# Both halves of a first operand over two hardware queues, and a new written order

## The chip, the cores and the metric

One core of a Trainium2 chip runs the kernel. The metric is the device time of one execution in microseconds (us). The times below are of eleven runs of the kernel before; one of them was also profiled.

## The reference

The reference is a two-step attention followed by a feed-forward layer. With q, k and v of 8 batches, 8 heads, 576 rows and 64 columns, and 32 packed rows p in each head:

```python
p_packed = softmax(p @ k.T / 8) @ v          # 32 rows per head
attn = softmax(q @ p_packed.T / 8) @ p_packed # 576 rows per head
x = attn, heads side by side                  # 4608 x 512
h = x @ w_in                                  # 512 -> 2048
out = (s * relu(h) ** 2 + b) @ w_out          # 2048 -> 512
```

Inputs and output are float32 in DRAM; the kernel's matmuls work on bf16.

## The kernel before

Inputs come in through DMAs. POOL's queue casts float32 to bf16 on the way. For each batch the work on TensorE (PE) is: transposes of k, q and p by matmuls with an identity (for later batches DMA transposes issued by SP); first scores (`s`), whose exponentials (`e`, on ACT) are the first softmax; the packed product (`a`, tile `pp`, copied to `ppc` on DVE); second scores (`c`) with their exponentials; their sums and reciprocals (`w`: matmuls with ones, then Ln and Exp on ACT as `ld` and `rcd`, then a product on DVE into `aT`); the product of the packed rows and w_in (`e`, `f`, `E`: four concurrent column groups, then scaled copies into `pw`, one half by ACT and one by DVE for `e`, both by DVE for `f`); the first layer (`h` and `m`: matmuls of `pw` and `aT`, Relu on ACT into `rlu`, square on DVE into `gT`); and the second layer (`t`: two of the 16 matmuls that add up one output tile of 128 rows, `yps`, which DVE copies into `ysb` with the factor and the bias, and SP stores).

The first three batches are not a loop. A string, `ORDER`, lists words by hand, and a dictionary, `words` (line 732 and after), says what each does. An instruction keeps its place on its engine (`tc.keep_in_program_order`), so the string sets the order on PE, ACT, DVE, POOL and SP. A word with numbers names the batch and the part: `kT.0.1` is the transpose of the second half of k of batch 0, `h.0.4` one of sixteen half results of the first layer of batch 0, `t.3` two matmuls of output tile 3, `win.0` the two DMAs of one quarter of w_in, `wout.0` one of w_out, `qh.0.0` two DMAs of q. `z` is an idle matmul: 128x512 zeros into a PSUM tile that nobody reads (`idle`, line 234). `pp2` doubles p in SBUF, `mask` makes the identity on POOL, `k.1`, `q.1`, `v.1` load later batches.

`four` and `three` change how PSUM is shared. At first there are two rings of two tiles, each two banks. From `four` on one ring holds four running sums (three output tiles and the sum of w_out, words `b`), and the other serves everything else. At `three` both rings are closed and replaced by three tiles of two banks and two of one bank for the output. After the string comes a loop over batches 3 to 7, with later loads, transposes and packed work at fixed steps.

Batch 0's k is loaded in two ways. Its first half (heads 0 to 3) is word `kf`: SP's hardware queue brings it as float32 into a corner of `gT`, which is not used yet, and word `kc` casts it, two heads by DVE and two by ACT. Its second half is `kh.0.1`, cast on the way by POOL's queue:

```python
    def load_first_k():
        kn[0] = raw("kn", 0).rearrange("r (h x) -> r h x", h=H)
        sp.dma_start(out=first_k, in_=k[0, 0:4].rearrange("h (r c) d -> r h (c d)", c=NC))
    def cast_first_k():
        vec.tensor_copy(out=kn[0][:, 0:2, :], in_=first_k[:, 0:2, :])
        act.copy(out=kn[0][:, 2:4, :], in_=first_k[:, 2:4, :])
```

Line 104 is the helper through which DVE, ACT, POOL and SP issue everything, line 93 that of matmuls and line 96 that of transposes, so the profile's groups are told apart by their tiles.

Of the kernel before, what the change touches and what calls it, by code (L numbers as in the profile page):

```python
# [7 lines left out]
F32 = mybir.dt.float32  # L8
# [4 lines left out]


ORDER = """
z kf kc kh.0.1 mask p.0.1 qh.0.0 qh.0.1 kT.0.1 kT.0.0 z z v.0 z win.0 win.1 pp2.0.1 pT.0 qT.0.1 z
s.0.0 s.0.1 qT.0.0 win.2 a.0.0 a.0.1 c.0.0 f.0.0 z win.3 c.0.1 z w.0.0 z w.0.1 e.0.1 z z h.0.2 h.0.0
e.0.2 wout.0 q.1 h.0.4 h.0.7 h.0.5 e.0.3 h.0.6 h.0.8 wout.1 h.0.1 h.0.11 h.0.13 k.1 h.0.3 four
h.0.10 t.1 p.1.2 h.0.9 wout.2 t.2 h.0.15 qT.1.1 t.1 t.2 qT.1.0 b.0 t.0 h.0.12 t.0 v.1 b.1 pp2.1.2
t.1 kT.1.1 t.2 pT.1 wout.3 sb b.2 h.0.14 q.2 kT.1.0 t.1 t.0 t.0 b.3 s.1.0 s.1.1 t.0 t.1 k.2 t.1  # L20
p.2.8 a.1.0 b.4 a.1.1 q.3 b.5 b.6 b.7 c.1 t.1 t.0 t.1 e.1.0 w.1.0 t.0 t.0 w.1.1 v.3 t.2 qT.2.1 t.2
e.1.1 k.3 t.2 t.2 t.2 kT.2.0 pp2.2.8 m.1.0 three t.3 t.3 pT.2 kT.2.1 f.1.2 t.3 e.1.3 v.2 t.3 qT.2.0
t.3 m.1.8 m.1.1 m.1.6 m.1.14 m.1.13 m.1.3 t.3 m.1.5 m.1.10 qo.3 m.1.2 t.4 qD.3 s.2.0 m.1.7 m.1.9
m.1.11 t.4 s.2.1 m.1.4 m.1.12 kD.3 t.3 m.1.15 a.2.0 t.4 a.2.1 t.4 t.4 t.4 pT.3 k.4 c.2 t.4 t.4 t.3
E.2.0 w.2.0 t.6 t.6 t.5 w.2.1 t.6 t.5 t.5 vo.3 t.6 E.2.1 t.6 m.2.5 t.5 t.5 t.6 pT.4 t.6 s.3.0 s.3.1
t.6 m.2.1 t.5 m.2.3 a.3.0 m.2.13 t.5 m.2.10 a.3.1 t.7 q.4 t.7 t.7 c.3 t.5 qo.4 m.2.2 t.7 t.7 w.3.0
t.8 t.8 E.3.0 qD.4 t.8 t.8 kD.4 w.3.1 v.4 t.7 m.2.14 t.7 m.2.0 m.2.15 m.2.6 m.2.7 m.2.9 t.8 t.8
m.2.12 m.2.8 m.2.11 t.7 m.2.4 E.3.1 t.8 t.8 vo.4
"""

@with_exitstack
def kernel(
# [19 lines left out]
    nc = tc.nc  # L52

    B, H, S, D = q.shape
# [6 lines left out]
    R = 96  # L61
    NC = S // R
# [43 lines left out]
    vec, act, pool, sp = (Pinned(e) for e in (nc.vector, nc.scalar, nc.gpsimd, nc.sync))  # L106
# [8 lines left out]
    kn, qn, vn = {}, {}, {}  # L115
# [7 lines left out]
    def raw(name, b):  # L123
        if (name, b - 1) in mine and b > 3:
            mine[name, b] = mine[name, b - 1]
        else:
            mine[name, b] = spare.pop(0)
        return bufs[mine[name, b]][:]
# [32 lines left out]
    def load_chunks(store, src, b, tag, hf):  # L161

        if hf == 0:
            store[b] = raw(tag, b).rearrange("r (h x) -> r h x", h=H)
        w = CP * D
        pool.dma_start(
            out=store[b][:, :, hf * w:(hf + 1) * w],
            in_=src[b].rearrange("h (r c) d -> r h (c d)", c=NC)[:, :, hf * w:(hf + 1) * w],
        )
# [3 lines left out]
    gT = wpool.tile([P, NFF, 3 * S], BF16, name="gT")  # L173
# [16 lines left out]
            in_=moe_w_out[m0 * P:m1 * P, :].rearrange("(m p) d -> p m d", p=P),  # L190
        )

    first_k = gT[0:R, 0:2, :].rearrange("p m s -> p (m s)")[:, 0:8 * NC * D].bitcast(F32)
    first_k = first_k.rearrange("r (h x) -> r h x", h=4)

    def load_first_k():

        kn[0] = raw("kn", 0).rearrange("r (h x) -> r h x", h=H)
        sp.dma_start(out=first_k, in_=k[0, 0:4].rearrange("h (r c) d -> r h (c d)", c=NC))

    def cast_first_k():
        vec.tensor_copy(out=kn[0][:, 0:2, :], in_=first_k[:, 0:2, :])
        act.copy(out=kn[0][:, 2:4, :], in_=first_k[:, 2:4, :])


    identb = constp.tile([P, P], BF16, name="identb")
# [2 lines left out]
    vec.memset(zeros[:], 0.0)  # L209
    svec = constp.tile([P, 1], F32, name="svec")  # L210
    bvec = constp.tile([P, 1], F32, name="bvec")
    nc.scalar.preload_act_table_set("natural_log_exp_and_others")
    KW = H * HS + 32
    kT = [constp.tile([P, KW], BF16, name=f"kT{i}") for i in range(2)]
    qT = [constp.tile([P, NC, HP, R], BF16, name=f"qT{i}") for i in range(2)]
# [511 lines left out]
    def constants():  # L727
# [9 lines left out]
        "qh": lambda b, x: load_pairs(qn, q, b, "qn", x),  # L737
        "vh": lambda b, x: load_pairs(vn, v, b, "vn", x),
        "qc": lambda b, x: load_chunks(qn, q, b, "qn", x),
        "kf": load_first_k,  # L740
        "kc": cast_first_k,
        "p": lambda b0, b1: load_p(b0, min(b1, B)),
        "win": load_w_in,
# [33 lines left out]
    for b in range(3, B):  # L777
        a = b + 1
        c = a + 1
# [61 lines left out]
```

The softmax here doesn't subtract the row's maximum and nothing guards it: scores larger than these inputs give would overflow.

## Time and profile before

| | us |
|---|---|
| median of 11 runs | 254.76 |
| lowest and highest | 254.37, 256.61 |
| the profiled execution | 256.38 |
| its span | 254.60 |
| PE busy | 242.0 (95%) |
| DVE busy | 145.7 (57%) |
| ACT busy | 143.6 (56%) |
| POOL busy | 32.9 (13%) |

Eight of the eleven times lie between 254.37 and 254.98, three between 256.10 and 256.61. The profiled execution is one of the three. Its time is 1.78 us more than its span, which is the part that the profile shows.

A busy PE is not a PE at its peak: the page counts an instruction as busy from its start to its modelled end, whatever the clock. The row PEclk gives the granted clock in tenths of full speed. A row of the chain of waits gives a start, a length and the work that ran or was waited for. In the timeline a bracket at the end of a row gives the idle time of its engine ahead of it, and what ended it.

### The profile page before, as it was taken

What the parts mean: (1) busy time and instruction counts of PE and PEld (TensorE: products, weight loads), DVE (VectorE), ACT (ScalarE), POOL (GpSimd) and SP (SyncE); (2) the same over time, 40 slices, a digit from 0 to 9 for tenths busy, and PEclk for the clock granted to TensorE, in tenths of its full rate; (3) what the DMA queues carried; (4) which work ended last, traced back from release to release, by engine and by line L of the source; (5) the groups of instructions that cost most, each with busy time, mean ns of one, the idle gap of its engine ahead of it and who ended that gap; (6) DMA issues with size and microseconds to landing.
All of it is one profiled execution on the core that took longest, in us unless ns stands there. A gap on an engine that the chain in (4) does not pass through costs nothing.

```text
span 254.6 us, 5632 instructions
## 1 busy us (share of the span) xinstructions
PE 242.0 (95%) x2330; PEld 138.0 (54%) x2330; DVE 145.7 (57%) x301; ACT 143.6 (56%) x220; POOL 32.9 (13%) x49
## 2 busy tenths in 40 slices
PE   0789999999999999999999999999999999999994
PEld 0554665456745656655566555645565555555443
DVE  3345843498757568667844677367834564454221
ACT  3058943457946698758663775568645764543000
POOL 8745242100003001100020013000000000000000
PEclk9986999999999999999999999999999999999999
DMA  7999999999499976995899499918511113111332
GB/s 142 194 202 205 205 204 194 196 234 209 83 122 163 215 138 113 169 232 121 154 138 223 103 172 147 213 47 157 115 41 44 41 47 82 41 41 41 85 82 82
DMA packets 54634, 34.61 MB, mean 136 GB/s; under 512 B 27344, under 2 KB 50128, under 8 KB 54608
## 3 DMA queue, kind: packets, MB, share of 16 engines
q0 software_dynamic: 24928, 18.32, 48.5%
q1 hardware_dynamic: 29584, 15.87, 27.7%
q8 instruction: 18, 0.29, 0.5%
q14 instruction: 8, 0.07, 0.1%
q10 hardware_dynamic: 96, 0.07, 0.1%
HBM read 37.23 MB, written 9.44 MB: 183 GB/s over the span
## 4 chain that ended last, share of the span: by engine, by line
PE 92%; DMA 3%; ACT 2%; DVE 1%; issue 1%; POOLq 0%
PE yps L93 51%; PE hps L93 37%; PE hps L96 3%; DMA raw<-in_k_dram 3%; ACT rlu L104 1%; ACT e L104 1%; DVE ysb L104 0%; ACT pw L104 0%; DVE pw L104 0%; DVE ppc L104 0%; POOLq L104 0%; POOLq L825 0%
## 5 line engine op out<-in xcount | busy, mean ns | idle before, releaser
L93 PE MATMUL yps<-w_out_sb,gT 128*128 128x512 bf16 (+2 forms) x592 | 144.6, 374 | 0.2 <-DVE ysb L104 0.2
L104 ACT ACTIVATE rlu<-hps 128x576 bf16<-128x576 f32 x128 | 80.6, 654 | 58.3 <-PE hps L93 52.1
L104 DVE TENSOR_TENSOR gT<-rlu 128x576 bf16<-128x576 bf16 x128 | 58.3, 457 | 56.9 <-ACT rlu L104 54.8
L93 PE MATMUL hps<-aT,pw 128*128 128x288 bf16 x512 | 80.2, 287 | 0.3 <-DVE pw L104 0.2
L93 PEld LDWEIGHTS <-gT 128*128 128x128 bf16 x592 | 53.5, 98 | 49.7 <-issue 7.2
L93 PEld LDWEIGHTS <-pw 128*128 128x128 bf16 x512 | 49.8, 98 | 32.2 <-issue 0.8
L104 DVE SCALAR_TENSOR_TENSOR ysb<-yps,svec,biasrep 128x512 f32<-128x512 f32 (+2 forms) x37 | 27.0, 732 | 16.5 <-PE yps L93 16.4
L104 DVE TENSOR_SCALAR pw<-hps,rd 128x1024 bf16<-128x1024 f32 (+1 forms) x22 | 22.6, 1037 | 1.0 <-PE hps L93 0.4
L104 ACT ACTIVATE pw<-hps,rd 128x1024 bf16<-128x1024 f32 (+1 forms) x18 | 17.5, 975 | 3.8 <-PE hps L93 3.7
L104 DVE TENSOR_TENSOR aT<-e,rcd 128x576 bf16<-128x576 bf16 x16 | 12.1, 758 | 11.1 <-ACT rcd L104 11.0
L104 POOL DMA_DIRECT2D raw<-in_k_dram x8 | 6.3, 782 | 87.9 <-DMA kT<-raw 62.8
L104 ACT ACTIVATE e<-hps,rs 128x576 bf16<-128x576 f32 (+1 forms) x18 | 11.4, 686 | 10.7 <-PE hps L93 8.7
L96 PE MATMUL hps<-identb,raw 96*64 96x96 bf16 (+1 forms) x216 | 9.5, 224 | 6.0 <-DMA raw<-in_k_dram 6.0
L104 ACT ACTIVATE e<-hps 96x768 bf16<-96x768 f32 x16 | 12.5, 801 | 3.9 <-PE hps L93 3.9
L96 PEld LDWEIGHTS <-raw 96*64 96x64 bf16 (+1 forms) x216 | 8.1, 117 | 8.8 <-DMA raw<-in_k_dram 6.5
L93 PE MATMUL hps<-w_in_sb,ppc 64*32 64x512 bf16 x256 | 11.2, 397 | 0.1
L104 ACT ACTIVATE rcd<-ld 128x576 f32<-128x576 f32 x16 | 11.0, 685 | 0.5
L104 ACT ACTIVATE ld<-hps 128x576 f32<-128x576 f32 x16 | 10.3, 643 | 1.0 <-PE hps L93 0.9
L104 DVE COPY raw<-raw 96x1536 bf16<-96x1536 bf16 x20 | 10.4, 562 | 0.0
L93 PEld LDWEIGHTS <-raw 96*64 96x64 bf16 (+1 forms) x264 | 7.7, 106 | 2.7 <-issue 2.0
L93 PE MATMUL hps<-e,raw 96*64 96x32 bf16 (+1 forms) x264 | 8.7, 188 | 0.4 <-ACT e L104 0.4
L104 POOL DMA_DIRECT2D raw<-in_q_dram x11 | 8.5, 784 | 4.0 <-PE hps L93 2.5
(45 smaller groups left out, 105.3 us busy)
## 6 DMA issues: line engine op xcount, KB each, us to landing
raw<-in_v_dram POOLq DMA_DIRECT2D x8, 576.0 KB, 11.6
out_dram<-ysb SPq DMA_DIRECT2D x23, 192.0 KB, 3.4
raw<-in_q_dram POOLq DMA_DIRECT2D x7, 576.0 KB, 11.0
raw<-in_k_dram POOLq DMA_DIRECT2D x7, 576.0 KB, 8.9
out_dram<-ysb SPq DMA_DIRECT2D x24, 128.0 KB, 2.4
w_in_sb<-in_moe_w_in_dram POOLq DMA_DIRECT2D x8, 256.0 KB, 10.0
w_out_sb<-in_moe_w_out_dram POOLq DMA_DIRECT2D x4, 512.0 KB, 15.2
out_dram<-ysb SPq DMA_DIRECT2D x23, 64.0 KB, 3.1
```

Source lines behind the costliest of these rows:

```text
L93: return tc.keep_in_program_order(nc.tensor.matmul(*a, **kw))
L96: return tc.keep_in_program_order(nc.tensor.transpose(*a, **kw))
L104: return lambda *a, **kw: tc.keep_in_program_order(f(*a, **kw))
```

## The change

Both halves of batch 0's k are loaded as float32, the first by SP's hardware queue and the second by ACT's, into two corners of `gT`. The two loads are issued ahead of all other words, and ahead of the load of ACT's table. The cast becomes a word with a half, `kc.0` and `kc.1`, each with one DVE and one ACT instruction. `kf` and `kh.0.1` are gone from the string. The string is otherwise a new order of the same words, with three `z` instead of ten, and with `e.1.2 f.1.3` instead of `f.1.2 e.1.3` (another quarter of `pw` is scaled by DVE alone).

```diff
 ORDER = """
-z kf kc kh.0.1 mask p.0.1 qh.0.0 qh.0.1 kT.0.1 kT.0.0 z z v.0 z win.0 win.1 pp2.0.1 pT.0 qT.0.1 z
-s.0.0 s.0.1 qT.0.0 win.2 a.0.0 a.0.1 c.0.0 f.0.0 z win.3 c.0.1 z w.0.0 z w.0.1 e.0.1 z z h.0.2 h.0.0
+p.0.1 mask qh.0.0 kc.0 qh.0.1 pp2.0.1 kc.1 kT.0.1 pT.0 kT.0.0 qT.0.1 v.0 win.0 s.0.0 z s.0.1 z
+qT.0.0 a.0.0 a.0.1 f.0.0 c.0.0 win.1 w.0.0 c.0.1 win.2 w.0.1 e.0.1 h.0.0 h.0.2 win.3 wout.0 e.0.2
...
-p.2.8 a.1.0 b.4 a.1.1 q.3 b.5 b.6 b.7 c.1 t.1 t.0 t.1 e.1.0 w.1.0 t.0 t.0 w.1.1 v.3 t.2 qT.2.1 t.2
-e.1.1 k.3 t.2 t.2 t.2 kT.2.0 pp2.2.8 m.1.0 three t.3 t.3 pT.2 kT.2.1 f.1.2 t.3 e.1.3 v.2 t.3 qT.2.0
+a.1.0 a.1.1 b.5 k.3 t.1 c.1 pp2.2.8 b.6 b.7 t.0 t.1 e.1.0 w.1.0 t.2 t.0 kT.2.1 w.1.1 t.0 v.3 t.0
+qT.2.0 t.2 e.1.1 t.2 t.2 m.1.0 three pT.2 kT.2.0 pT.3 v.2 t.3 e.1.2 t.3 qT.2.1 t.3 f.1.3 m.1.1 t.3
...
     def load_first_k():
 
         kn[0] = raw("kn", 0).rearrange("r (h x) -> r h x", h=H)
-        sp.dma_start(out=first_k, in_=k[0, 0:4].rearrange("h (r c) d -> r h (c d)", c=NC))
+        for x, queue in enumerate((sp, act)):
+            queue.dma_start(
+                out=first_k[x], in_=k[0, 4 * x:4 * x + 4].rearrange("h (r c) d -> r h (c d)", c=NC)
+            )
 
-    def cast_first_k():
-        vec.tensor_copy(out=kn[0][:, 0:2, :], in_=first_k[:, 0:2, :])
-        act.copy(out=kn[0][:, 2:4, :], in_=first_k[:, 2:4, :])
+    def cast_first_k(x):
+        vec.tensor_copy(out=kn[0][:, 4 * x:4 * x + 2, :], in_=first_k[x][:, 0:2, :])
+        act.copy(out=kn[0][:, 4 * x + 2:4 * x + 4, :], in_=first_k[x][:, 2:4, :])
+
+    load_first_k()
+    nc.scalar.preload_act_table_set("natural_log_exp_and_others")
...
-    nc.scalar.preload_act_table_set("natural_log_exp_and_others")
```

More of the change, by code (lines that the diff above doesn't have):

```diff
@@ L15 @@
 ORDER = """
-z kf kc kh.0.1 mask p.0.1 qh.0.0 qh.0.1 kT.0.1 kT.0.0 z z v.0 z win.0 win.1 pp2.0.1 pT.0 qT.0.1 z
-s.0.0 s.0.1 qT.0.0 win.2 a.0.0 a.0.1 c.0.0 f.0.0 z win.3 c.0.1 z w.0.0 z w.0.1 e.0.1 z z h.0.2 h.0.0
-e.0.2 wout.0 q.1 h.0.4 h.0.7 h.0.5 e.0.3 h.0.6 h.0.8 wout.1 h.0.1 h.0.11 h.0.13 k.1 h.0.3 four
-h.0.10 t.1 p.1.2 h.0.9 wout.2 t.2 h.0.15 qT.1.1 t.1 t.2 qT.1.0 b.0 t.0 h.0.12 t.0 v.1 b.1 pp2.1.2
-t.1 kT.1.1 t.2 pT.1 wout.3 sb b.2 h.0.14 q.2 kT.1.0 t.1 t.0 t.0 b.3 s.1.0 s.1.1 t.0 t.1 k.2 t.1
@@ L21 @@
-p.2.8 a.1.0 b.4 a.1.1 q.3 b.5 b.6 b.7 c.1 t.1 t.0 t.1 e.1.0 w.1.0 t.0 t.0 w.1.1 v.3 t.2 qT.2.1 t.2
-e.1.1 k.3 t.2 t.2 t.2 kT.2.0 pp2.2.8 m.1.0 three t.3 t.3 pT.2 kT.2.1 f.1.2 t.3 e.1.3 v.2 t.3 qT.2.0
-t.3 m.1.8 m.1.1 m.1.6 m.1.14 m.1.13 m.1.3 t.3 m.1.5 m.1.10 qo.3 m.1.2 t.4 qD.3 s.2.0 m.1.7 m.1.9
-m.1.11 t.4 s.2.1 m.1.4 m.1.12 kD.3 t.3 m.1.15 a.2.0 t.4 a.2.1 t.4 t.4 t.4 pT.3 k.4 c.2 t.4 t.4 t.3
-E.2.0 w.2.0 t.6 t.6 t.5 w.2.1 t.6 t.5 t.5 vo.3 t.6 E.2.1 t.6 m.2.5 t.5 t.5 t.6 pT.4 t.6 s.3.0 s.3.1
@@ L26 @@
-t.6 m.2.1 t.5 m.2.3 a.3.0 m.2.13 t.5 m.2.10 a.3.1 t.7 q.4 t.7 t.7 c.3 t.5 qo.4 m.2.2 t.7 t.7 w.3.0
-t.8 t.8 E.3.0 qD.4 t.8 t.8 kD.4 w.3.1 v.4 t.7 m.2.14 t.7 m.2.0 m.2.15 m.2.6 m.2.7 m.2.9 t.8 t.8
-m.2.12 m.2.8 m.2.11 t.7 m.2.4 E.3.1 t.8 t.8 vo.4
+p.0.1 mask qh.0.0 kc.0 qh.0.1 pp2.0.1 kc.1 kT.0.1 pT.0 kT.0.0 qT.0.1 v.0 win.0 s.0.0 z s.0.1 z
+qT.0.0 a.0.0 a.0.1 f.0.0 c.0.0 win.1 w.0.0 c.0.1 win.2 w.0.1 e.0.1 h.0.0 h.0.2 win.3 wout.0 e.0.2
+e.0.3 q.1 h.0.7 wout.1 h.0.4 h.0.10 h.0.15 h.0.9 z four h.0.8 k.1 h.0.1 wout.2 t.0 h.0.12 p.1.2
@@ new lines @@
+h.0.5 b.0 qT.1.0 t.2 v.1 h.0.3 t.1 h.0.6 wout.3 h.0.13 t.2 sb t.1 h.0.11 h.0.14 b.1 t.0 pp2.1.2 t.1
+b.2 qT.1.1 t.1 t.2 pT.1 b.3 kT.1.0 kT.1.1 t.0 p.2.8 t.0 k.2 q.2 s.1.0 q.3 s.1.1 t.1 t.1 b.4 t.2
+a.1.0 a.1.1 b.5 k.3 t.1 c.1 pp2.2.8 b.6 b.7 t.0 t.1 e.1.0 w.1.0 t.2 t.0 kT.2.1 w.1.1 t.0 v.3 t.0
+qT.2.0 t.2 e.1.1 t.2 t.2 m.1.0 three pT.2 kT.2.0 pT.3 v.2 t.3 e.1.2 t.3 qT.2.1 t.3 f.1.3 m.1.1 t.3
+m.1.9 t.3 m.1.14 m.1.5 m.1.2 m.1.6 qo.3 m.1.13 qD.3 m.1.3 t.4 s.2.0 s.2.1 t.3 m.1.15 kD.3 t.4 m.1.12
+m.1.7 k.4 m.1.11 m.1.10 t.3 m.1.4 m.1.8 a.2.0 t.3 a.2.1 t.4 q.4 pT.4 t.4 t.4 vo.3 c.2 t.4 t.4 t.4
@@ L29 @@
+t.5 E.2.0 t.5 t.6 s.3.0 t.6 w.2.0 t.5 t.6 w.2.1 t.6 E.2.1 t.5 s.3.1 t.5 t.6 t.6 m.2.1 t.6 m.2.3 t.6
+m.2.4 a.3.0 m.2.5 a.3.1 m.2.13 t.7 t.5 t.5 c.3 t.7 t.7 t.5 qo.4 m.2.14 m.2.2 t.7 w.3.0 t.7 t.8 m.2.0
+qD.4 v.4 m.2.10 kD.4 m.2.9 t.8 m.2.6 m.2.12 t.7 m.2.8 E.3.0 t.8 t.8 t.8 w.3.1 m.2.7 t.8 E.3.1 t.8
+t.7 m.2.11 t.7 t.8 m.2.15 vo.4
 """
@@ L191, in load_w_out @@
         )
-    first_k = gT[0:R, 0:2, :].rearrange("p m s -> p (m s)")[:, 0:8 * NC * D].bitcast(F32)
-    first_k = first_k.rearrange("r (h x) -> r h x", h=4)
+    first_k = [
+        gT[0:R, 2 * x:2 * x + 2, :].rearrange("p m s -> p (m s)")[:, 0:8 * NC * D].bitcast(F32).rearrange(
+            "r (h x) -> r h x", h=4
+        )
+        for x in range(2)
+    ]
     def load_first_k():
         kn[0] = raw("kn", 0).rearrange("r (h x) -> r h x", h=H)
-        sp.dma_start(out=first_k, in_=k[0, 0:4].rearrange("h (r c) d -> r h (c d)", c=NC))
-    def cast_first_k():
-        vec.tensor_copy(out=kn[0][:, 0:2, :], in_=first_k[:, 0:2, :])
-        act.copy(out=kn[0][:, 2:4, :], in_=first_k[:, 2:4, :])
+        for x, queue in enumerate((sp, act)):
+            queue.dma_start(
+                out=first_k[x], in_=k[0, 4 * x:4 * x + 4].rearrange("h (r c) d -> r h (c d)", c=NC)
+            )
+    def cast_first_k(x):
[3 more added lines that the diff above has]
+    nc.scalar.preload_act_table_set("natural_log_exp_and_others")
     identb = constp.tile([P, P], BF16, name="identb")
@@ L739 @@
         "qc": lambda b, x: load_chunks(qn, q, b, "qn", x),
-        "kf": load_first_k,
         "kc": cast_first_k,
```

## The prediction

> **What bounds the kernel now.** I read the page's busy slices first, to see which engine is full and when; then the chain of waits through the first 25 us; then one-microsecond windows for the clock; then the timeline around 54 us, where the order of words changes most after the opening.
>
> ```profile
> PE   0789999999999999999999999999999999999994
> DVE  3345843498757568667844677367834564454221
> PEclk9986999999999999999999999999999999999999
> ```
>
> Each digit is a slice of 6.4 us, PE is full from the third slice to the last, and the clock row has one dent, in slices three and four.
>
> ```profile
> 1.29 6.50 DMA raw<-in_k_dram
> 7.84 2.10 PE hps L96 x24
> 9.94 1.28 PE hps L93 x3
> ...
> 15.15 1.50 PE hps L93 x59
> ...
> 17.02 1.83 PE hps L93 x20
> 18.87 0.90 ACT e L104 x2
> 19.82 3.93 PE hps L93 x18
> 23.77 1.19 ACT rlu L104 x2
> ```
>
> The chain (start, length, what) begins with the second half of k, cast on its way by POOL's queue, and PE's first transposes wait for it until 7.84. The piece of 1.28 us "x3" is three idle matmuls. From 17.02 to 23.77 PE and ACT hand over to each other: this is latency, not throughput.
>
> ```profile
> core 0: us, PE busy (x) PEld busy (x) DVE busy (x) ACT busy (x) POOL busy (x), PEclk, DMA share, GB/s
> 16.00:17.00 1.00, 0.63 (x30) 0.51 (x26) 0.45 (x3) 0.00 (x0) 0.54 (x2) 0.82 1.23 203
> 22.00:23.00 1.00, 1.00 (x4) 0.21 (x3) 0.65 (x1) 0.97 (x2) 0.73 (x1) 0.50 1.22 202
> 24.00:25.00 1.00, 0.94 (x14) 0.51 (x13) 0.94 (x3) 1.00 (x3) 0.36 (x1) 1.00 1.23 205
> 50.00:60.00 10.00, 10.00 (x131) 5.30 (x130) 9.23 (x17) 5.51 (x9) 0.77 (x1) 1.00 1.31 237
> ```
>
> The clock is half from 16.65 (a share of 0.82 in that window) to about 23.5. Loads run at 200 GB/s without a break. From 50 to 60 us DVE is busy 9.23 of 10, the only stretch in which it is as full as PE.
>
> ```profile
> 53.62 0.75 DVE L104 TENSOR_SCALAR pw<-hps,rd 128x512 bf16<-128x512 f32 x1
> 54.29 0.74 DVE L104 SCALAR_TENSOR_TENSOR ysb<-yps,svec,biasrep 128x512 f32<-128x512 f32 x1
> 54.58 0.66 PE L93 MATMUL hps<-aT,pw 128*128 128x288 bf16 x4
> 54.95 0.75 DVE L104 COPY kT<-hps 128x1152 bf16<-128x1152 bf16 x1
> 55.09 1.02 PE L93 MATMUL yps<-w_out_sb,gT 128*128 128x512 bf16 x4
> 56.02 0.29 PE L96 MATMUL hps<-identb,pn 128*128 128x128 bf16 x2
> ```
>
> This is the word `three`: the eviction of the last early output tile ends at 55.03, the first matmul in the new PSUM pools starts at 55.09, and m.1.0 (54.58) covers the time until then. PE loses nothing, but with no slack.
>
> **What the Trainium skill says.** "TensorE: Matmul & The Clock Gate", Part 1, "What's actually happening": the array runs at half rate unless it was busy over a window of about 3.4 us, and the windows run on their own. The trace agrees: the half rate lasts 6.8 us, two windows, and idle matmuls of 512 columns start 0.43 us apart at 9.74 to 11.01, the half rate, although no event is recorded that early; transposes of q fall from 42 ns apart at 11.4 to 23 ns at 13.9. "DMA: Bandwidth & Descriptors", "Issuing engines are not separate DMA queues": queues of several engines share the same 16 DMA engines and only issue time is saved. The trace before can't show two hardware queues loading together; POOL's 200 GB/s written is 400 GB/s read. Same page, "Specifications": the first byte takes 0.6 us on a hardware queue, 1 us on POOL's. Here it is later: SP issues at 0.74 and its packets begin after 1.5; POOL issues at 1.29 and its packets begin after 3.5.
>
> **Part 1, k by two hardware queues.** Removed: POOL's issue for half of k (0.81 us) and its cast on the way. Added: one issue on ACT (about 0.4 us, as SP's 0.39), ahead of the table load (1.28 us, now ending at about 2.4 and needed at the first cast: no cost), one DVE cast (0.56) and one ACT cast (0.83). SP's half alone lands at 5.1 and its rate climbs to 350 GB/s. Two halves are 1.18 MB, 3.4 us at that rate, after the start at 1.6 and a slow first microsecond: I take both landed at 5.9, bounds 5.3 and 7.2. The casts stand one behind the other: ACT 2 x 0.8, DVE 0.5 + pn's copy 0.2 + 0.5, done at 7.5. pn's copy now waits on DVE for p's landing, and the second cast is queued behind it, then kT's eviction, for which PE's scores wait; p is now POOL's first issue (1.29 instead of 2.43), so I put p at 5.5 and this wait at nothing; if p came at 7, the casts end at 7.8. The first transposes start at about 7.1 instead of 7.84.
>
> They no longer decide. prep_q_chunks needs all of q, and q's last load (issue 5.3, landing 5.9 later, 11.2) released qT.0.1 at 11.36. POOL issues q 0.8 us earlier with less ahead of it, but the bytes before it are the same: I take 10.4, bounds 10.0 and 11.1. v lands at 13.8 instead of 14.5, w_in's chunk 0 at 16.2 instead of 16.9 by the same shift.
>
> **Part 2, the opening's order.** Ten idle matmuls become three; five of those removed ran at 0.43 us in the cold stretch. Working forward: qT.0.1 10.5 to 11.5; s.0.0 without the idle matmul ahead of it; two e of 0.8 and a qT copy of 0.64 on ACT, done at 13.7; a.0.0 at 13.9 (15.15 before); a takes 1.5, ppc 0.35: 15.8. Now f.0.0 stands ahead of c.0.0 and waits for chunk 0 until 16.2, 0.43 at half rate, then c.0.0 at 16.65 (17.02 before) and e at 17.1 (17.68 before). Gain so far 0.6.
> Then ACT's chain. Before: four e, w.0.0's matmuls, ld, rcd, ld, rcd, from 17.68 to the pw at 23.02, 5.34 us, with one hand-over to PE. After: e e (0.9), w.0.0 (0.6), ld (0.65), rcd (0.6), e e (0.9), w.0.1 (0.6), ld (0.65), rcd (0.6) = 5.5, with two. w.0.1 stands ahead of h.0.0 on PE, so the first half's early aT helps little. From that pw on ACT is full until about 31 (20 results of h and e), so the gain there is the gain of the opening: **0.4 us**, bounds -0.5 (k at 7.2) and 1.2. No load is late: wout.0 landed at 26.9, first used at 30.4; later ones had 1 to 3 us.
>
> **Part 3, the switch.** Words before `three` were `e.1.1 k.3 t.2 t.2 t.2 kT.2.0 pp2.2.8 m.1.0 three t.3 t.3 pT.2`; they become `e.1.1 t.2 t.2 m.1.0 three pT.2 kT.2.0 pT.3`. kT.2.1 moves ahead of w.1.1, so one kT eviction (step 0.67) comes before the last ysb on DVE, which was already full. No work is added for PE; it stands elsewhere. Of what covered DVE's queue after e.1.1, one t.2 (0.43) is done earlier, and the last ysb comes 0.67 later, with no slack to absorb either: 1.1 us of PE waiting, for e.1.1's pw and for that ysb. The four t.3 matmuls (0.9) that stood behind the switch and needed only one bank are gone from there; pT.2, kT.2.0, pT.3 all need DVE's evictions (0.56 + 0.67 + 0.56). I take **1.0 us lost**, bounds 0 and 1.6.
>
> **Part 4, the clock.** A stretch with waits between short matmuls drops a window: 13.2 to 16.65 did, with about 0.6 of it streaming. After the change the same share holds in the stretch of the switch, and, without idle matmuls, at 24 to 27 us where PE waits for pw. One more half-rate window costs at most 3.41/2 = 1.7 us; where DVE or ACT bounds it, less. I take **1.0**, bounds 0 and 2.7.
>
> **Edits at nothing:** swapping e.1.3/f.1.2 for e.1.2/f.1.3 (one eviction from ACT to DVE and one back); later loads and the DMA transposes, reordered on POOL and SP, are hidden behind PE's full stretch from 70 us; if a transpose came late, s.3 would wait, and 5 us of landing is the price.
>
> Sum: -0.4 + 1.0 + 1.0 = +1.6. The profiled execution took 256.38 us with a span of 254.60, which is 1.6 above the median of 254.76, about one half-rate window; on its terms the result is 258.0, against the median **256.4**. I expect the same difference for both.
>
> **Rivals.** (a) **Faster.** The loads decide: if both halves land by 5.3 and the whole stream of loads comes 1 us early, f.0.0 finds its weights at 15.9, e starts at 16.7, the gain is 0.4 + 0.4, and 0.2 more if pw's waits on PE go; if m.1.0 still covers the switch nothing is given back: 253.8. For it speak 6.5 us of the first chain piece on k, and that only 0.27 MB had moved by 3.0. Against it speaks that the same 16 engines are full from there on. It decides from a landing of v under 13.5. (b) **No change.** Opening +0.4 against a switch of 0.4 to 1.0 and no lost window: 254.8 to 255.4. (c) **Two queues slow each other** and POOL's small packets of p; k lands at 7.2, PE starts at 8.4, the gain is zero and windows are lost twice: 258.2. (d) The change not doing what it says: the built order shows ACT's load ahead of its table load and both casts, so it does.
>
> **Numbers.** Forecast 0.55, (c) 0.15, (a) 0.14, (b) 0.16, (d) under 0.01; so slower 0.70, faster 0.14, same 0.16, where 0.3%, about what a measurement of this kernel can tell from no change, is 0.76 us. Range 254.2 to 258.2: rival (b) and nearly all of (c) are inside; the forecast's own range is 255.5 to 258.2.
>
> **What would show it.** Right: k landing near 5.9; qT.0.1 near 10.5; rlu near 23.4; PE waiting on DVE around 55 us; PEclk under 1.00 near 25 or 57 us. Wrong: no wait at 55 us, or a clock row with only the first dent; v landing under 13.5.

## The result, and the profile after

The changed kernel takes 256.97 us (median of 13 runs, 256.66 to 257.55). The kernel before, run beside it, takes 254.99 us (median of 50 runs); the ratio is 1.007, with a 95% interval of 1.0051 to 1.0088. So it is slower by 1.3 to 2.2 us. Its profiled execution took 256.77 us with a span of 255.0.

The busy slices of the page of the changed kernel (the first three rows that were shown of before):

```profile
PE   0768999989999999999999999999999999999994
DVE  2545743597775577767844678367834574454221
PEclk9997999999999999999999999999999999999999
```

PE reaches a 9 one slice later than before (in the fifth slice instead of the fourth), and has a new 8 in slice nine (51.0 to 57.4 us). The clock row still has one dent, in slice four, and none near 57 us.

The chain of waits up to the first place where PE is the bound (start, length, what):

```profile
2.49 2.45 POOL raw L104 x4
4.94 7.78 DMA raw<-in_v_dram
12.72 0.28 issue
13.01 11.30 DMA w_in_sb<-in_moe_w_in_dram
24.30 0.04 issue
24.35 1.74 PE hps L93 x17
```

The chain no longer runs over k and ACT. It runs along POOL's queue: four loads of q are issued, v lands at 12.72 (before, it landed near 14.5, from the issue at 5.83 and 8.7 us to landing), and w_in's last quarter lands only at 24.30, when PE is already waiting for it. "4.94 7.78" is issue and time to landing.

The windows that were shown of before:

```profile
16.00:17.00 1.00, 0.53 (x16) 0.24 (x17) 0.75 (x4) 0.15 (x1) 0.54 (x1) 1.00 1.24 205
22.00:23.00 1.00, 1.00 (x6) 0.50 (x4) 0.85 (x2) 1.00 (x3) 0.69 (x1) 0.50 1.23 203
24.00:25.00 1.00, 0.65 (x10) 0.37 (x10) 0.85 (x2) 0.76 (x2) 0.85 (x2) 1.00 1.25 208
50.00:60.00 10.00, 9.15 (x127) 4.86 (x127) 8.52 (x17) 5.34 (x9) 0.77 (x1) 1.00 1.27 235
```

The columns are window, length, busy time of PE, PE's weight load, DVE, ACT and POOL, then clock, DMA share and GB/s. In 24:25 PE stood still for 0.35 us (0.94 busy before, 0.65 now), and in 50:60 it lost 0.85 us (10.00 before). The clock there is 1.00.

The timeline at the switch of the PSUM pools:

```profile
54.25 0.65 PE L93 MATMUL hps<-aT,pw 128*128 128x288 bf16 x4
54.81 0.74 DVE L104 SCALAR_TENSOR_TENSOR ysb<-yps,svec,biasrep 128x512 f32<-128x512 f32 x1
54.94 0.65 ACT L104 ACTIVATE rlu<-hps 128x576 bf16<-128x576 f32 x1 [0.83 <-PE hps L93]
55.70 0.27 PE L96 MATMUL hps<-identb,pn 128*128 128x128 bf16 x2 [0.80 <-ACT rlu L104]
55.80 0.67 PE L96 MATMUL hps<-identb,raw 96*128 96x96 bf16 x12
```

m.1.0 ends at 54.90. The last early output tile is evicted until 55.55 and m.1.0 itself until 55.59. pT.2, the first word in the new pools, comes behind both and starts at 55.70 (the profile names ACT's rlu here, and DVE's ysb for the same place in a run below). PE waits 0.80 us where it waited nothing before.

The loads of the opening, issue to landing (KB each, median us):

```profile
gT<-in_k_dram ACTq DMA_DIRECT2D x1, 576.0 KB, 6.5
gT<-in_k_dram SPq DMA_DIRECT2D x1, 576.0 KB, 5.9
pn<-in_p_dram POOLq DMA_DIRECT2D x1, 32.0 KB, 6.3
```

Both k loads are issued at 0.74, so k is there at 6.6 and 7.2. Before, SP's half alone took 4.4 us.

### The profile page after: what moved, and what is told of

The parts are those of the page before. It is cut to its first block, busy times and chain, and to the rows that moved or that the text cites. A ratio compares the mean times of both kernels' runs of the same rounds, so it can differ in the third digit from the quotient of the medians.

```text
span 255.0 us, 5620 instructions
## 1 busy us (share of the span) xinstructions
PE 239.1 (94%) x2323; PEld 137.4 (54%) x2323; DVE 145.9 (57%) x302; ACT 145.3 (57%) x221; POOL 31.8 (12%) x48
## 4 chain that ended last, share of the span: by engine, by line
PE 88%; DMA 7%; POOL 1%; ACT 1%; issue 0%; DVE 0%; POOLq 0%
PE yps L93 51%; PE hps L93 35%; DMA w_in_sb<-in_moe_w_in_dram 4%; DMA raw<-in_v_dram 3%; PE hps L96 2%; POOL raw L104 1%; POOL pn L104 0%; ACT pw L104 0%; ACT rlu L104 0%; ACT ld L104 0%; DVE ysb L104 0%; POOL identb L104 0%; POOLq L104 0%; POOLq L833 0%
## 5 line engine op out<-in xcount | busy, mean ns | idle before, releaser
L93 PE MATMUL hps<-aT,pw 128*128 128x288 bf16 x512 | 81.1, 288 | 0.0
L104 POOL DMA_DIRECT2D raw<-in_k_dram x7 | 5.4, 778 | 90.1 <-DMA kT<-raw 84.5
L96 PEld LDWEIGHTS <-raw 96*64 96x64 bf16 (+1 forms) x216 | 8.1, 116 | 11.1 <-DVE raw L104 8.3
L93 PEld LDWEIGHTS <-ppc 64*32 64x32 bf16 x384 | 3.8, 89 | 10.3 <-issue 7.2
L93 PE MATMUL hps<-e,onesbd 128*128 128x288 bf16 x32 | 7.0, 289 | 2.4 <-ACT e L104 2.2
L93 PEld LDWEIGHTS <-kT 128*128 128x128 bf16 x192 | 8.0, 102 | 1.7 <-issue 0.3
```

The source lines that it names most:

```text
L93: return tc.keep_in_program_order(nc.tensor.matmul(*a, **kw))
L96: return tc.keep_in_program_order(nc.tensor.transpose(*a, **kw))
L104: return lambda *a, **kw: tc.keep_in_program_order(f(*a, **kw))
```

## The experiments

Two places in the order can be compared exactly, as all kernels have done the same work on PE there, except for idle matmuls (some have issued loads of batch 2 earlier): the first scores of batch 1 (word `s.1.0`, seen as the third e of 96 partitions), and `m.1.0`, the last word ahead of `three` (seen as the seventeenth rlu; of batch 2, one k half and one q half are transposed by then in each). The table gives their times in the profiled execution of each run, with the first rlu and the end of the last instruction. Kernels are named by the labels of their runs.

| kernel | first rlu | s.1.0 | m.1.0 | end | m.1.0 to end | ratio to before (95%) |
|---|---|---|---|---|---|---|
| before | 23.77 | 42.19 | 55.27 | 254.60 | 199.33 | 1 |
| b_again (before) | 22.96 | 41.38 | 54.46 | 253.80 | 199.34 | 0.9993 (0.9975 to 1.0012) |
| e_k_alone | 22.62 | 41.03 | 54.12 | 253.34 | 199.22 | 1.0009 (0.9985 to 1.0032) |
| e_c_first | 22.57 | 41.13 | 54.22 | 253.54 | 199.32 | 0.9997 (0.9979 to 1.0014) |
| e_open_new | 23.21 | 42.12 | 55.20 | 254.51 | 199.31 | 1.0019 (1.0004 to 1.0035) |
| after | 22.59 | 41.80 | 54.94 | 255.00 | 200.06 | 1.0070 (1.0051 to 1.0088) |
| e_order_alone | 23.55 | 42.48 | 55.61 | 255.72 | 200.11 | 1.0073 (1.0046 to 1.0100) |
| e_z | 23.21 | 41.95 | 55.09 | 255.14 | 200.05 | 1.0052 (1.0034 to 1.0070) |
| e_switch | 23.36 | 42.53 | 55.92 | 255.63 | 199.72 | 1.0067 (1.0046 to 1.0089) |
| e_tail_old | 22.68 | 41.67 | 55.92 | 255.29 | 199.37 | 1.0069 (1.0043 to 1.0095) |
| e_tail_old_b | 23.80 | 42.90 | 56.31 | 255.69 | 199.37 | 1.0060 (1.0039 to 1.0082) |
| e_both | 23.46 | 44.33 | 57.74 | 257.12 | 199.38 | 1.0128 (1.0104 to 1.0153) |
| e_tail_new | 22.46 | 40.88 | 60.83 | 260.77 | 199.94 | 1.0188 (1.0133 to 1.0243) |
| e_tail_new_b | 22.44 | 40.85 | 54.64 | 254.84 | 200.20 | 1.0106 (1.0082 to 1.0130) |

The last column but one is the clean one: from m.1.0 to the end the words of before take 199.2 to 199.4 us in eight profiles, and those of the change 199.9 to 200.2 in five (e_switch, which puts two words back, lies between). The columns before it vary from execution to execution, with the landing of k and with the clock.

### The kernel before once more (b_again)

No edit. It asks what the two groups of times of before are.

> The kernel before, profiled again, with the granted clock of each run. My theory: its times fall in two groups (254.1 to 255.1 and 255.5 to 256.8) because a run has one or two half-rate windows of 3.4 us in its first 25 us, so the runs near 254.7 show a mean clock near 0.993 and a span near 252.9, those near 256.3 a clock near 0.987 and a span near 254.6. Rival: the groups have nothing to do with the clock; then both show the same clock, and what makes them is elsewhere in the span.

255.65 us, ratio 0.9993. The profile shows the same two half-rate windows as the first one, and yet everything is 0.81 us earlier from the first rlu to the end. The lists of PE's waits tell why, first the kernel before, then its second run (total, times, longest):

```profile
PE hps L96 <- DMA raw<-in_k_dram: 6.0, 1, 6.0
```

```profile
PE hps L96 <- DMA raw<-in_k_dram: 4.9, 1, 4.9
```

POOL's half of k landed 1.1 us earlier. So this landing has a part in the groups, as far as two profiles can tell. The clock has a share too: of 39 executions of before beside these runs, the 12 with a mean granted clock of 1.000 had spans of 253.1 us on average, the 15 with 0.987 had 254.35. The changed kernel's 14 executions lie between 0.984 and 0.993.

### The switch undone (e_switch)

```diff
-w.1.0 t.2 t.0 kT.2.1 w.1.1
+w.1.0 t.2 t.0 w.1.1
...
-t.2 t.2 m.1.0 three pT.2 kT.2.0 pT.3 v.2 t.3 e.1.2 t.3 qT.2.1 t.3
+t.2 t.2 kT.2.1 m.1.0 three t.3 t.3 pT.2 kT.2.0 pT.3 v.2 e.1.2 qT.2.1 t.3
```

> The changed kernel with one place put back as it was: kT.2.1 stands right ahead of m.1.0 again, and two t.3 right behind three. My theory: the 0.80 us that PE idles at 55 us goes, and with it 0.8 to 1.0 us of the time, to about 256.0. Rival 1: the wait only moves to the next word that needs DVE's evictions, and the time stays within 0.3 of 257.0. Rival 2: the wait makes a half-rate window in some runs; then the gain is over 1.5.

257.27 us, ratio 1.0067 (1.0046 to 1.0089): no gain is seen at the median, where one of 0.8 to 1.0 us was expected. In the profile PE does not wait at the switch, but it does 3 us later, in the timeline:

```profile
57.69 0.76 DVE L104 COPY kT<-hps 128x1152 bf16<-128x1152 bf16 x1
58.50 0.70 PE L96 MATMUL hps<-identb,raw 96*64 96x96 bf16 x24 [0.38 <-DVE kT L104]
```

The two t.3 that moved to the switch had stood around e.1.2, ahead of qT.2.1, and without them PE meets DVE's queue there. From m.1.0 to the end it gains 0.34 of 0.75 us, which is too little for this interval to show. So two t.3 cover one wait or the other, not both: the rival's mechanism, in part.

### The loads alone and the order alone (e_k_alone, e_order_alone)

The old order with the new loads:

```diff
-z kf kc kh.0.1 mask
+z kc.0 kc.1 mask
```

> The old order of words with the new loads of k alone (both halves as float32 on the two hardware queues ahead of everything, two casts each on DVE and ACT; kf and kh.0.1 gone). My theory: k is ready at 8.2 instead of 7.8, but q and v come 0.7 and 1.7 us earlier as in the changed kernel, and the order's idle matmuls eat most of it: 0 to 0.5 us faster than before. Rival: the loads are what costs; then it is 1 us or more slower than before, and POOL's starved queue shows it.

The new order with the old loads:

```diff
-p.0.1 mask qh.0.0 kc.0 qh.0.1 pp2.0.1 kc.1 kT.0.1
+kf kh.0.1 p.0.1 mask qh.0.0 kc qh.0.1 pp2.0.1 kT.0.1
```

> The new order of words with the old loads of k (SP's half as float32, the other half first on POOL's queue). My theory: the order is what costs: slower than before by 2.0 to 3.0 us, so slower than the changed kernel by 0 to 1, since v lands 1.7 us later. Rival: the order costs nothing by itself; then it is within 0.5 of before.

The loads alone give 255.39 us, ratio 1.0009 (0.9985 to 1.0032): no difference is seen, neither the gain that was expected nor the rival's loss of 1 us. The order alone gives 257.76 us, ratio 1.0073 (1.0046 to 1.0100), as much as the whole change: the loss is the order's, to within 0.7 us. The fair base for the change's order is therefore e_k_alone, and against it the changed kernel's profile loses 0.8 us by s.1.0 and 0.8 us more behind m.1.0.

### Heads and tails exchanged at e.1.0 (e_tail_old, e_tail_new)

Each is the head of one order up to e.1.0 (46 us), and then the remaining words in the other one's order.

```diff
-b.6 b.7 t.0 t.1 e.1.0 w.1.0 t.2 t.0 kT.2.1 w.1.1
+b.6 b.7 t.0 t.1 t.0 e.1.0 w.1.0 t.0 t.0 w.1.1
...
-m.1.0 three pT.2 kT.2.0 pT.3 v.2 t.3 e.1.2
+m.1.0 three t.3 t.3 pT.2 kT.2.1 f.1.2 t.3 e.1.3
```

> The changed kernel's words up to c.1 and the words around it (46 us), and from e.1.0 on the words of the kernel before in the order of before. Theory (the loss has two parts, 0.7 to 0.8 us before 42 us and 0.9 us between 50 and 55 us, against the old order with the new loads): the second part goes, the wait of 0.8 us after `three` is gone and nothing of it comes back later; 0.9 below the changed kernel, ratio to before 1.003 to 1.004. Rival (the loss belongs to the opening, as PE's missing idle matmuls and a lower clock, and whatever stands at the switch is made up for elsewhere, as the run with only the switch undone suggests): no change against the changed kernel, ratio 1.007.

257.13 us, ratio 1.0069 (1.0043 to 1.0095). The wait at `three` is gone, but the seam has one of its own: t.0 now stands right behind the last t.1, with which it shares a PSUM tile, and PE waits 0.84 us at 48.24 for that tile's eviction. The ratio is the rival's, but with a new wait as long as the old one it decides nothing.

The mirror image:

```diff
-c.1 t.1 t.0 t.1 e.1.0 w.1.0 t.0 t.0 w.1.1
+c.1 t.1 t.0 t.1 t.2 k.3 pp2.2.8 e.1.0 w.1.0 t.2 kT.2.1 w.1.1
```

> The mirror image: the old order with the new loads up to c.1, and the changed kernel's words from e.1.0 on. Theory: it loses only the second part, 0.9 us, ratio to before 1.0035 to 1.0045, with a wait of PE near 54 us behind DVE or ACT. Rival: nothing is lost by the tail (ratio 1.000 to 1.002), or all of it (1.007).

260.91 us, ratio 1.0188 (1.0133 to 1.0243), and no answer either: kT.2.1, which stands early in the new tail, waits 2.5 us for k.2, which the old head issues late. It shows what else belongs to the moved word: the loads of batch 2 had to move with it.

### The opening alone, in two lengths (e_open_new, e_c_first)

e_open_new keeps the change up to e.0.1 (without the later idle matmuls), e_c_first only up to a.0.1; then the order of before follows.

```diff
 w.0.0 c.0.1 win.2 w.0.1 e.0.1
-h.0.0 h.0.2 win.3 wout.0 e.0.2 e.0.3 q.1 h.0.7 wout.1 h.0.4 h.0.10 h.0.15
+win.3 h.0.2 h.0.0 e.0.2 wout.0 q.1 h.0.4 h.0.7 h.0.5 e.0.3 h.0.6 h.0.8
```

> The changed kernel's words up to e.0.1 (22 us), without further idle matmuls, then the order of before from h.0.2 h.0.0 e.0.2 on, so e.0.2, e.0.3 stand among the h again, and the middle, the switch and the rest are those of before. Theory: what is lost before 42 us is lost between 23 and 30 us, where e.0.2 and e.0.3 stand ahead of the h and the second of them waits for w_in's last quarter, so this one keeps up with the old order with the new loads: first rlu within 0.2 us of it, ratio to before 1.000 to 1.002. Rival (the two waits of PE for e, 0.62 and 1.60 us, and the missing idle matmuls are the loss): ratio 1.003 to 1.004, and no execution with a full clock.

255.82 us, ratio 1.0019 (1.0004 to 1.0035): 0.5 us lost, with 0.1 to 0.9 in the interval. The ratio is the theory's, at its upper end, and the interval holds the rival's too. No execution of it reached a mean clock of 1.000 (0.984 to 0.993), as the rival said; its first rlu is 0.59 us later than that of e_k_alone, not within 0.2.

```diff
 qT.0.0 a.0.0 a.0.1
-f.0.0 c.0.0 win.1 w.0.0 c.0.1 win.2 w.0.1 e.0.1
+win.1 win.2 c.0.0 f.0.0 z win.3 c.0.1 z w.0.0 z w.0.1 e.0.1 z z
```

> The changed kernel's opening up to a.0.1 only, then the order of before: c.0.0 f.0.0 z c.0.1 z w.0.0 z w.0.1 e.0.1 and all that follows. Theory (the opening gains 0.4 us up to the first second scores against the old order with the new loads, and loses it again by w.0.0 standing ahead of c.0.1, for PE waits 1.60 us for the second pair of e there): the gain stays, first rlu 0.3 to 0.5 us before that of the old order with the new loads, ratio to before 0.997 to 0.999. Rival (the weights' landing or a half-rate clock takes it back by 25 us): ratio 1.000 to 1.002.

254.87 us, ratio 0.9997 (0.9979 to 1.0014): level with before, the rival's number, and the one version with words of the change for which no loss is seen. The first words of the change are harmless to within 0.4 us; its profile has a full clock throughout, and a first rlu that is level with that of e_k_alone although PE started at 8.80 against 8.07.

### The idle matmuls put back (e_z)

```diff
-a.0.1 f.0.0 c.0.0 win.1 w.0.0 c.0.1 win.2 w.0.1
+a.0.1 z f.0.0 c.0.0 win.1 z w.0.0 c.0.1 win.2 z z z w.0.1
```

> The changed kernel with five idle matmuls put back where PE waits in the opening (one ahead of f.0.0, one ahead of w.0.0, three ahead of w.0.1). If the missing idle matmuls keep the clock down (no execution of the changed kernel had a mean clock over 0.993, a third of before's had 1.000), some executions reach 1.000 and the median falls by 0.5 to 0.8 us, ratio to before 1.004 to 1.005. Rival (a loss of clock there costs nothing, since PE waits for ACT and DVE in those windows): the same as the changed kernel, 1.007, or 0.2 us more where an idle matmul ends later than the wait that it fills.

256.92 us, ratio 1.0052 (1.0034 to 1.0070). The clock part of the theory holds: five of nine executions had a mean clock of 1.000. The time part is open. The ratio lies just above the theory's 1.004 to 1.005, but its interval overlaps that of the changed kernel. Within this run the five executions at 1.000 have spans of 255.1 us on average, and the three at 0.991 and 0.992 of 255.2: the full clock by itself was worth little. The clock row of the page, and the timeline ahead of e.0.3:

```profile
PEclk9999999999999999999999999999999999999999
```

```profile
22.69 0.41 PE L93 MATMUL hps<-w_in_sb,ppc 64*32 64x512 bf16 x8
22.77 0.76 DVE L104 TENSOR_TENSOR aT<-e,rcd 128x576 bf16<-128x576 bf16 x1 [1.76 <-ACT rcd L104]
23.45 0.74 DVE L104 TENSOR_SCALAR pw<-hps,rd 128x512 bf16<-128x512 f32 x1
24.24 0.46 PE L93 MATMUL hps<-w_in_sb,ppc 64*32 64x512 bf16 x8 [1.14 <-DVE pw L104]
```

The first row is e.0.2, the last e.0.3. At full rate PE is ready for e.0.3 at 23.10 and stands still, now not for w_in but for a PSUM tile: DVE's part of e.0.1's pw waits behind aT, and aT behind ACT. In the changed kernel, at half rate until 23.58, PE waits 0.35 us there, for w_in, and e.0.3 starts at 24.35. The idle matmuls bought a clock, and a longer wait ahead of e.0.3 took back most of what PE had gained there.

### The old tail with a clean seam, and e.0.3 later (e_tail_old_b, e_both)

```diff
-t.0 t.1 t.0 e.1.0 w.1.0 t.0 t.0 w.1.1 v.3 qT.2.1 t.2 e.1.1 t.2 t.2 t.2 kT.2.0
+t.0 t.1 e.1.0 w.1.0 t.2 t.0 t.0 w.1.1 v.3 t.0 qT.2.1 t.2 e.1.1 t.2 t.2 kT.2.0
```

> The changed kernel's words up to t.0 t.1 (46 us) and the tail of before from e.1.0 on, as in the earlier run of that kind, but with the words at the seam ordered so that t.0 doesn't stand right behind the end of t.1, whose output tile shares its PSUM tile (PE waited there 0.84 us for an eviction): e.1.0 w.1.0 t.2 t.0 t.0 w.1.1 v.3 t.0 qT.2.1 t.2 e.1.1 t.2 t.2 kT.2.0 m.1.0 three t.3 t.3 pT.2 kT.2.1. Theory (0.9 us of the loss belongs to the words from e.1.0 on): no wait at the switch, 0.7 to 0.9 us below the changed kernel, ratio to before 1.003 to 1.004. Rival (DVE's evictions are too many for that stretch in any order that comes to it from this head): a wait of 0.5 to 1 us for DVE in another place between 48 and 60 us, ratio 1.006 to 1.007.

256.70 us, ratio 1.0060 (1.0039 to 1.0082): the rival's number. In the profile it takes 199.37 us from m.1.0 on, as the old orders do, so what is lost behind the switch is gone, as the theory said. One wait of 0.36 us for DVE's copy of qT appears ahead of m.1.0 instead, a part of what the rival said. That would leave a gain of 0.4 us, an estimate from the two figures, and the median, 0.25 us lower by the ratios, can't tell it from none.

The same with e.0.3 later:

```diff
-e.0.2 e.0.3 q.1 h.0.7 wout.1 h.0.4 h.0.10 h.0.15
+e.0.2 q.1 h.0.7 wout.1 h.0.4 h.0.10 e.0.3 h.0.15
```

> The last kernel with e.0.3 moved behind three of the h (e.0.2 q.1 h.0.7 wout.1 h.0.4 h.0.10 e.0.3 h.0.15). Theory: e.0.3 no longer waits for w_in's last quarter (0.35 us in the changed kernel, 1.1 us where idle matmuls kept the clock full) and ACT's and DVE's pw stand closer to the h that they serve; 0.3 to 0.7 us are gained between 23 and 31 us, and the end is as much lower than the last kernel's; ratio to before 1.000 to 1.002. Rival (the stretch to 31 us is PE's and ACT's work in either order, and the weights' landing is only a place where the wait shows): no gain by 31 us.

258.53 us, ratio 1.0128 (1.0104 to 1.0153): a miss. (The wait of 1.1 us which its expectation puts down to w_in was that of e_z for DVE's pw, as shown above.) The wait for w_in is gone, but PE now waits 0.98 us at 27.21 for ACT's pw and 0.49 us at 28.49 for DVE's, as h.0.15 needs e.0.3's pw right behind it. What e.0.3 costs at its place in the change is not settled by this edit.

### The new tail with its loads in time (e_tail_new_b)

```diff
-b.2 h.0.14 q.2 kT.1.0 t.1
+b.2 h.0.14 kT.1.0 p.2.8 k.2 q.2 t.1
...
-c.1 t.1 t.0 t.1 e.1.0 w.1.0 t.0 t.0 w.1.1
+c.1 t.1 t.0 t.1 t.2 pp2.2.8 e.1.0 w.1.0 t.2 kT.2.1 w.1.1
```

> The old order with the new loads up to c.1 and the changed kernel's words from e.1.0 on, as in the earlier run of that kind, but with p.2.8 and k.2 issued ahead of q.2 and k.3 behind q.3, so that kT.2.1 and pp2.2.8 find their data (PE waited 2.5 us for k there and DVE's pn until 52.9). What was done by the first scores of batch 1 and by `three` is then the same set of words in both kernels. Theory (0.8 us of the loss lies at and behind `three` and comes with any head): level with the old order at the first scores of batch 1 (41 us), 0.7 to 0.9 us behind it from the end of batch 1 on; ratio to before 1.003 to 1.005. Rival (the wait at the switch only shows where the changed kernel's own head has filled DVE's queue): under 0.3 us, ratio 1.000 to 1.002. If a load is still late there, it shows as a wait for a DMA near 50 us, and the run tells nothing.

257.76 us, ratio 1.0106 (1.0082 to 1.0130), above what theory and rival gave. The median is no measure of the switch: q.2 is late here (0.2 us of waiting in the profile), the seam adds a wait of 0.57 us at 49.00, and most executions have spans 1 us or more above that of the profile. The profile, one execution, speaks for the theory. Level with e_k_alone at s.1.0 (0.18 ahead), it needs 200.20 us from m.1.0 to the end, like the changed kernel, with a head that is wholly the old one. Its timeline at the switch:

```profile
54.60 0.74 DVE L104 SCALAR_TENSOR_TENSOR ysb<-yps,svec,biasrep 128x512 f32<-128x512 f32 x1
54.64 0.65 ACT L104 ACTIVATE rlu<-hps 128x576 bf16<-128x576 f32 x1 [0.74 <-PE hps L93]
55.49 0.27 PE L96 MATMUL hps<-identb,pn 128*128 128x128 bf16 x2 [0.89 <-DVE ysb L104]
```

The same wait, 0.89 us, and here the profile names the eviction of ysb. In the changed kernel it named ACT's rlu: the two end within 0.04 us of each other there, so either name stands for the pair.

## Why the prediction was right, and where it was not

The forecast of 256.4 us, a loss, and the range hold. The sum of +1.6 us meets a measured +1.8, and that closeness is in good part luck: of its three terms one was right in size, the opening was too low by 1.4 us, and the 1.0 us set down for lost clock windows, which did not come, stood in for it.

**The opening, forecast -0.4: wrong in sign.** In the pair of profiles s.1.0 comes 0.39 us earlier, as forecast, but in the profile of before k had landed late; b_again has the same words 0.42 us earlier than the changed kernel. By ratios the whole loss is 1.8 us, the switch has 0.75 of it, and so the words ahead of it about +1.0. Up to a.0.1 no loss is seen (0.9997), up to e.0.1 0.5 us (0.1 to 0.9). The profiles agree, if more than a pair is taken: four runs have the change's words up to s.1.0 without an edit, and three have the old words with the new loads.

| words up to s.1.0, with the new loads | second scores' first e to first pw | first rlu | first rlu to s.1.0 | s.1.0 |
|---|---|---|---|---|
| of the change (after, e_switch, e_tail_old, e_tail_old_b) | 5.16 to 5.28 | 22.59 to 23.80 | 18.99 to 19.21 | 41.67 to 42.90 |
| of before (e_k_alone, e_tail_new, e_tail_new_b) | 4.77 to 4.86 | 22.44 to 22.62 | 18.41 to 18.42 | 40.85 to 41.03 |

The change's words are later at s.1.0 by 1.3 us on average, and by 0.6 us at the least. Four parts of the forecast's step failed:

- **The landing of k**: forecast 5.9, bounds 5.3 to 7.2; landed 6.6 and 7.2. The sum took SP's peak rate for both halves.
- **The wait for p, put at nothing.** On DVE the second cast stands behind pn's copy, and p landed at 7.55, not 5.5. PE's first transposes came at 8.27, not 7.1, and not earlier than the 7.84 of before. In the eight profiles with the change's first words and the new loads they come 1.5 to 1.8 us after the first cast begins; with both casts ahead of that copy (the three old-order profiles of the table) 1.2 to 1.3. By itself this cost nothing that shows: e_c_first has it too, at 0.9997. That the landing of k would no longer decide held: the first exponentials of batch 0 came at 12.47 against 13.60.
- **ACT's chain.** Forecast 5.5 against 5.34 in the profile of before, it took 5.2 (16.85 to 22.02). But that profile ran the whole chain at half rate, and the old order with the new loads needs 4.8. So with the same loads the change's order of these words, with its two hand-overs to PE, takes about 0.4 us more than the old one, and not 0.16. How much of that is the clock is not separated: e_z, at a full clock, takes 5.04. The first rlu at 22.59, earlier than the forecast 23.4, was the earliest of the four.
- **"The gain there is the gain of the opening."** This took ACT to be full until about 31 us, as it is in before (7.89 of 8 us from the first rlu on). In the changed kernel it is busy for 7.24 of the same 8 us, and from the first rlu to s.1.0 its words take 0.6 to 0.8 us longer. Why is open. "No load is late" was wrong: w_in's last quarter, which e.0.2 e.0.3 side by side ask for at 24 us, landed at 24.30. But of the four runs only the changed kernel shows that wait (0.35 us), and the half rate lasts for 1.0 us of that stretch in it (22.59 to 23.58) and for about 2.5 in e_switch and e_tail_old_b, at the same length. So neither can be the whole reason.

**The switch, forecast +1.0: right in size and place, the reason only in part.** The profiles with the change's words behind `three` take about 0.75 us more from m.1.0 on, with the old head (e_tail_new_b) as with the new, and five of the change's head or opening with the old words there do not (e_tail_old, e_tail_old_b, e_both, e_open_new, e_c_first). This rests on profiles: no kernel with the change's head and other words at the switch gets the 0.75 back at the median (1.0060 to 1.0069 in e_switch, e_tail_old and e_tail_old_b), as each has a new wait of PE elsewhere (0.38, 0.84 and 0.36 us).

Of the two waits that were forecast, that for e.1.1's pw did not come: m.1.0 starts at 54.25 while DVE still scales that quarter (54.14 to 54.89). The other was put down to DVE's last ysb alone, and m.1.0's own eviction was left out. In before, too, pT.2 starts only when that rlu has ended, at 55.92:

```profile
55.27 0.65 ACT L104 ACTIVATE rlu<-hps 128x576 bf16<-128x576 f32 x1 [1.68 <-PE hps L93]
```

pT.2 followed at 56.02, but two t.3 ran until then. In the changed kernel the rlu ends at 55.59, 0.04 us behind the ysb. So with an idle DVE the wait would have been about as long (an estimate from these ends; no run has it): what the change lost is mainly the cover of the two t.3. That part of the forecast, t.3 gone from behind the switch, was right. e_switch agrees: with the two t.3 back the wait is gone, and they are missed 3 us later.

**The clock, forecast +1.0: did not come.** No window was dropped at 55 us or at 24 to 27 us; the profile has one half-rate window and that of before two. The rule that a share of 0.6 drops a window, taken from 13.2 to 16.65, does not carry over to one wait of 0.80 in a full stretch. The clock may have a part in the opening instead, inside the +1.0 above: no execution of the changed kernel had a full clock, and five of nine had it with the idle matmuls put back. It is not a term that adds up, as e_z shows: with a full clock PE waited longer for DVE's pw. And the reading of before's two groups as one half-rate window was only half right (b_again).

**Two queues for one load.** The page "DMA: Bandwidth & Descriptors" of the Trainium skill, "Issuing engines are not separate DMA queues", has queues of several engines share the same 16 DMA engines, and this fits what the runs show: with two hardware queues each half took 5.9 and 6.5 us where SP's alone, beside POOL's queue, took 4.4, and with the loads alone no difference was seen at the median (1.0009). That they interleave, as the page has it, is not seen for POOL's queue in the first 6 us (last section).

**The rivals.** Rival (a), faster, made its decision depend on v landing under 13.5. v landed at 12.7 and e started at 16.85, near its 16.7, and the kernel was slower all the same: the loss lies behind these points, in ACT's chain, in the stretch behind the first rlu and at the switch. Rival (c) had k at 7.2 and PE's start at 8.4, which is close to what came (7.2 and 8.27), but no loss is seen from it (e_k_alone, e_c_first).

## What to carry to other kernels

Compare two orders of words where both have done the same set of words, and take the difference from there to the end: 0.75 us stood out here in single profiles, while everything ahead of it varied by 1 us with a landing and the clock. For what lies ahead of such a place, take several profiles of the same words: one pair showed a gain of 0.39 us where four against three showed a loss of 1.3.

A stage that ends in a change of PSUM pools needs, right behind it, matmuls that don't wait for the eviction of the word just ahead of it (here two t.3 covered m.1.0's rlu), and those matmuls are then missing where they stood. And a higher clock in an opening of many waits is worth only what the next wait leaves of it: with a full clock PE came to e.0.3 earlier and stood there for 1.14 us.

## What was unexpected of the hardware

- In the changed kernel POOL's queue moved nothing while two hardware queues loaded. For the first 6 us the list of queues holds only those two (packets, MB, share of 16 engines), and so it is in e_k_alone:

```profile
q1 hardware_dynamic: 400, 0.59, 34.1%
q10 hardware_dynamic: 358, 0.55, 32.8%
```

POOL's first load, p, of 32 KB, was issued at 1.25 and landed 6.3 us later; before, beside one hardware queue, POOL's queue had moved 0.25 MB by 6.0 us, and p, issued second, took 5.6.
- The landing of the same first loads differed by 1.1 us between two executions of the same kernel (6.0 against 4.9 us of PE's waiting), as much as the whole effect of the opening's order.
- In e_tail_new's profile the clock records show the half rate in mid-kernel, from 52.85 to 59.67 us. PE had waited there from 49.02 to 51.56 and again from 52.24 to 53.99 (2.54 and 1.75 us). In the profiles with a wait of 0.80 to 0.89 us in the same stretch the clock stayed at 1.00.
